# A cached-attention block whose transposing key loads are cut in two

## The chip, the cores and the metric

The kernel runs on one core of a Trainium2 chip. The metric is the device time of one execution in microseconds (us); lower is better. Three runs of the kernel before took 436.45, 436.83 and 437.62 us, with a median of 436.83 us.

On the core, TensorE (PE in the profile, with its weight loads as PEld) multiplies and transposes, VectorE (DVE) and ScalarE (ACT) work on what it leaves in PSUM, and SyncE (SP) issues every transfer between DRAM and SBUF. All transfers issued by SP run on the same 16 DMA engines.

## What is computed

Eight sequences of 112 queries attend to a cache of 512 keys and values, with 32 heads of 192 elements. Everything that is passed in is bf16.

```python
B, Sq, D = 8, 112, 640
H, Sk, Dh = 32, 512, 192
q = (x @ wq).reshape(B, Sq, H, Dh).transpose(0, 2, 1, 3)
scores = einsum("bhqd,bhkd->bhqk", q, k_cache) * Dh ** -0.5
p = softmax(scores, axis=-1)
o = einsum("bhqk,bhkd->bhqd", p, v_cache)
return o.transpose(0, 2, 1, 3).reshape(B, Sq, H * Dh) @ wo
```

The key cache and the value cache hold 8·32·512·192 elements each, 50 MB in bf16. They are read once and are most of what has to be moved.

## The kernel before

The work is cut into 32 tiles `i = 8r + b`: `r` is one of four groups of eight heads, `b` is the sequence. A tile has two steps, `n = 2i` for its first four heads and `n = 2i + 1` for the other four. `qd = n % 2` says which half a step is.

For each group of heads and each half of the batch, the `Q` operations project the queries with a piece of `wq`. Each step then runs: scores (`Sm` and `St`, line 773), the row minimum of the negated scores (`smax`, VectorE, line 830), the exponential (`exp`, ScalarE, line 835), the division by the row sum (`norm`, VectorE, line 839), the transpose of the probabilities on TensorE (`PT`, line 874), and the product with the values (`PVt` and `PVm`, lines 906 and 918). The `O` operations (line 940) multiply by a piece of `wo` and are summed in SBUF over the head groups.

For the scores the keys are needed with the 192 elements of a head on the partitions, which is not how the cache stores them. There are two ways to get there. The first seven tiles are loaded plainly (`KN`, line 189) and transposed on TensorE (`KT`, line 672). From tile 7 on, each tile of eight heads is one transposing transfer (`load_k`, line 158; in the profile `DMA_TRANSPOSE kt<-in_k_cache_dram`, 25 of them). It reads 1024 rows of 768 elements, 8·512·192·2 bytes = 1.57 MB, and writes six blocks of 1024 columns into one of `KS = 4` places of the buffer `kt`. Values come as plain copies, two to a tile with four heads each (`load_v`, line 167, 768 KB), into one of three places of `vt`. The pieces of `wq` (`WQ`, line 205, 480 KB) and `wo` (`WO`, line 216, 960 KB) are reloaded for each group of heads.

Nothing is scheduled at run time. `ORDER_PE`, `ORDER_ACT`, `ORDER_DVE` and `ORDER_SP` are lists written out in the source; each engine follows its list, and `Plan.run` puts a wait in front of an operation for each semaphore that its dependencies raise and that this engine has not waited for yet. What is late on one engine therefore holds up everything behind it in the same list.

Three rules decide when SP issues a load:

- The list `ORDER_SP`. In the part that matters it mixes keys, values and weights, often with two to four key tiles in a row: `('K', 21), ('K', 20), ('K', 22)`.
- The place. `k_place_free` makes the load of tile `i` wait for the scores of tile `i - 4`, for both of its steps, since that tile's keys lie in the place. Values wait for the product with the values three tiles earlier, weights for the operations that use their place last.
- A limit on how much is under way. Each load has a size (`size`, line 1104): a value half counts 0.5, a key tile 1.5, a `WQ` piece a third. A load waits until the latest load with at least `AHEAD = 0.95` issued behind it has landed.

On the other side, `scores(n)` waits with its first matmuls for the key load of tile `n // 2`, `PVt` for the value half of its step, `Q` for its `wq` piece.

Near the end, five steps (57 to 61) have their probabilities transposed by a transfer instead of by TensorE (`TD`, line 858).

Of the kernel before, what the change touches and what calls it, by code (L numbers as in the profile page):

```python
# [11 lines left out]
class Plan:  # L12
# [6 lines left out]
    def add(self, eng, name, deps, emit, sem=None, inc=1):  # L19
        assert name not in self.ops, name  # L20
        self.ops[name] = dict(eng=eng, deps=deps, banks=[], emit=emit, sem=sem, inc=inc)
# [31 lines left out]
def build_mha_kernel(nc, x, k_cache, v_cache, wq, wo, out):  # L53
# [4 lines left out]
    HU = 8  # L58
# [28 lines left out]
    with ExitStack() as es:  # L87
# [59 lines left out]
            return e.tensor_copy(dst, src)  # L147


        def k_place_free(i):  # L150
            return [s_last(2 * (i - KS) + 1)] if i >= KS else [("XT", c) for c in range(4)] if i == KS - 1 else []

        def load_k(i):
            r, b = divmod(i, B)

            def emit(e):
                src = k_cache[b, r * HU:(r + 1) * HU].rearrange("u (r q) d -> (u r) (q d)", q=4)
                return e.dma_start_transpose(kt[:, i % KS].rearrange("p a m c -> p (a m) c"), src)
            add("SP", ("K", i), k_place_free(i), emit, f"mK{i % KS}", 16)

        def load_v(i, half):
            r, b = divmod(i, B)
# [22 lines left out]
        def load_kn(i, lo, hi):  # L185

            def emit(e):
                b, h0 = i % B, i // B * HU
                return e.dma_start(kn[i][:, lo:hi, :], k_cache[b, h0 + lo:h0 + hi].rearrange("u (r q) d -> r u (q d)", q=4))
            if PLAIN[i] == "place":  # L190
                old = k_place_free(i)
            else:
                last = [k for k in homed(PLAIN[i]) if k < i][-1:]
                old = [("KT", k, p) for k in last for p in range(lo // 2, hi // 2)]
            add("SP", ("KN", i, lo, hi - lo), old, emit, f"mKN{i}_{lo}", 16)
            kn_of.update({(i, u): ("KN", i, lo, hi - lo) for u in range(lo, hi)})
# [33 lines left out]
        def s_last(n):  # L230
            return ("S2" if n in ROWS else "St", n, 1)

        def pv_all(n):
# [323 lines left out]
            ('KN', 0, 4, 4), ('KN', 1, 0, 4), ('KN', 1, 4, 4), ('KN', 2, 0, 4), ('KN', 2, 4, 4), ('V', 2, 0), ('V', 2, 1),  # L557
            ('V', 0, 0), ('V', 0, 1), ('WQ', 1, 0, 1), ('KN', 3, 0, 4), ('KN', 3, 4, 4), ('KN', 4, 0, 4), ('KN', 4, 4, 4),
            ('V', 1, 0), ('V', 1, 1), ('V', 3, 0), ('V', 3, 1), ('WQ', 1, 2, 1), ('WQ', 1, 1, 1), ('KN', 5, 0, 4),
            ('KN', 5, 4, 4), ('WQ', 1, 3, 1), ('KN', 6, 0, 4), ('KN', 6, 4, 4), ('V', 4, 0), ('V', 4, 1), ('K', 7),  # L560
            ('K', 8), ('WO', 0, 0), ('WO', 0, 1), ('V', 6, 0), ('V', 6, 1), ('V', 5, 0), ('V', 5, 1), ('V', 7, 0),
            ('V', 7, 1), ('K', 10), ('K', 9), ('V', 8, 0), ('V', 8, 1), ('K', 11), ('WQ', 2, 0, 1), ('V', 9, 0),
            ('V', 9, 1), ('V', 10, 0), ('V', 10, 1), ('K', 12), ('K', 13), ('V', 11, 0), ('V', 11, 1), ('K', 14),
            ('WQ', 2, 1, 1), ('WQ', 2, 2, 1), ('V', 12, 0), ('V', 12, 1), ('WQ', 2, 3, 1), ('WO', 1, 0), ('WO', 1, 1),
            ('V', 13, 0), ('V', 13, 1), ('K', 16), ('K', 15), ('V', 14, 0), ('V', 14, 1), ('V', 15, 0), ('V', 15, 1),
            ('K', 17), ('K', 18), ('K', 19), ('V', 16, 0), ('V', 16, 1), ('V', 17, 0), ('V', 17, 1), ('V', 18, 0),
            ('V', 18, 1), ('K', 21), ('K', 20), ('K', 22), ('WQ', 3, 0, 1), ('WQ', 3, 1, 1), ('V', 20, 0), ('V', 20, 1),
            ('WQ', 3, 2, 1), ('V', 19, 0), ('V', 19, 1), ('WQ', 3, 3, 1), ('WO', 2, 0), ('WO', 2, 1), ('V', 21, 0),
            ('V', 21, 1), ('V', 22, 0), ('V', 22, 1), ('K', 23), ('K', 25), ('K', 24), ('K', 26), ('V', 24, 0),
            ('V', 24, 1), ('V', 23, 0), ('V', 23, 1), ('V', 25, 0), ('V', 25, 1), ('K', 28), ('K', 27), ('K', 29),  # L570
            ('V', 27, 0), ('V', 27, 1), ('V', 26, 0), ('V', 26, 1), ('WO', 3, 0), ('WO', 3, 1), ('V', 28, 0), ('V', 28, 1),
            ('K', 30), ('K', 31), ('TD', 57), ('TD', 58), ('V', 29, 0), ('V', 29, 1), ('TD', 59), ('V', 30, 0),
            ('V', 30, 1), ('TD', 60), ('TD', 61), ('OUT', 3), ('OUT', 0), ('V', 31, 0), ('V', 31, 1), ('OUT', 5),
            ('OUT', 1), ('OUT', 2), ('OUT', 4), ('OUT', 6), ('OUT', 7)]
        BANKS = [
            (('XT', 0), 1), (('XT', 1), 4), (('XT', 3), 2), (('XT', 2), 3), (('Q', 0, 1, 1), 1), (('Q', 0, 0, 0), 5),
            (('Q', 0, 0, 1), 4), (('Q', 0, 1, 0), 6), (('KT', 0, 0), 4), (('KT', 0, 1), 0), (('Q', 0, 1, 2), 7),
# [88 lines left out]
        def k_transposes(i, p):  # L666
            bank = bank_of["KT", i, p]

            def emit(e):
                for y in range(12):  # L670
                    c, u = divmod(y, 2)
                    ends = [e.transpose(psb[:, bank + t, y * 64:(y + 1) * 64],  # L672
                                        kn[i][64 * t:64 * t + 64, 2 * p + u, c * 128:(c + 1) * 128],
                                        ident[64 * t:64 * t + 64, 64 * t:64 * t + 64]) for t in range(2)]
                return tuple(ends)

            add("PE", ("KT", i, p), [kn_of[i, 2 * p], kn_of[i, 2 * p + 1]], emit, ("PE", "PE2"))
            old = k_place_free(i) if PLAIN[i] != "place" else []
            for t in range(2):
                def evac(e, t=t):  # L680
                    dst = kt_pair(i, p).rearrange("p m (u t s) -> p m u t s", t=2, s=64)[:, :, :, t, :]
                    src = psb[:, bank + t, 0:768].rearrange("p (c u s) -> p c u s", c=6, u=2)
                    return copy(("evK", i, p, t), e, dst, src)
                add("DVE", ("evK", i, p, t), [("KT", i, p)] + old, evac)
# [82 lines left out]
        def scores(n):  # L767
# [8 lines left out]
            for j in range(2):  # L776
                def straight(e, j=j):
                    for h in range(2):
                        f = h == 0
                        if h == 0:  # L780
                            ev = [q_at(n, j, 0, 0, 64), q_at(n, j, 1, 0, 64)]
                            od = [h_at(n, j, 0, 64, 128), h_at(n, j, 1, 64, 128)]
                        else:
                            ev = [h_at(n, j, 2, 0, 64), h_at(n, j, 3, 0, 64)]
                            od = [q_at(n, j, 1, 64, 128), q_at(n, j, 2, 64, 128)]
                        for i in range(2):
                            a = mm(e, j, h, 0, ev[i], i, 0, 64, f and i == 0, False)
                            b = mm(e, j, h, 1, od[i], 1 + i, 64, 128, f and i == 0, False)
                    return a, b

                def swapped(e, j=j):
                    for h in range(2):
                        od, ev = ((h_at(n, j, 1, 0, 64), q_at(n, j, 0, 64, 128)) if h == 0 else
                                  (q_at(n, j, 2, 0, 64), h_at(n, j, 2, 64, 128)))
                        a = mm(e, j, h, 1, od, 2, 0, 64, False, True)
                        b = mm(e, j, h, 0, ev, 0, 64, 128, False, True)
                    return a, b

                def mains(e, j=j):
                    for h in range(2):  # L800
                        ev, od = ((q_at(n, j, 0, 0, 128), h_at(n, j, 1, 0, 128)) if h == 0 else
                                  (h_at(n, j, 2, 0, 128), q_at(n, j, 2, 0, 128)))
                        mm(e, j, h, 0, ev, 0, 0, 128, h == 0, False)
                        last = mm(e, j, h, 1, od, 2, 0, 128, h == 0, False)
                    return last

                def rests(e, j=j):
                    for h in range(2):
                        ev, od = ((q_at(n, j, 1, 0, 64), h_at(n, j, 0, 64, 128)) if h == 0 else
                                  (h_at(n, j, 3, 0, 64), q_at(n, j, 1, 64, 128)))  # L810
                        a = mm(e, j, h, 0, ev, 1, 0, 64, False, True)
                        b = mm(e, j, h, 1, od, 1, 64, 128, False, True)
                    return a, b
                keys = ([("evK", n // 2, 2 * qd + j, t) for t in range(2)] if n // 2 in PLAIN else [("K", n // 2)])
                if n in ROWS:
                    add("PE", ("S1", n, j), [("qc", n)] + keys, straight, ("PE", "PE2"))
                    add("PE", ("S2", n, j), [("S1", n, j)], swapped, ("PE", "PE2"))
                else:
                    add("PE", ("Sm", n, j), [("qc", n)] + keys, mains)
                    add("PE", ("St", n, j), [], rests, ("PE", "PE2"))  # L820
# [280 lines left out]

        def size(op):

            return {"V": 0.5, "WQ": op[-1] / 3, "KN": op[-1] / 8, "WO": 0.625, "K": 1.5, "X": 0.25, "TD": 0.5, "OUT": 0}[op[0]]

        for i, op in enumerate(ORDER_SP):
            behind = [k for k in range(i) if sum(map(size, ORDER_SP[k + 1:i])) >= AHEAD]
# [94 lines left out]
```

## Time and profile before

| | |
|---|---|
| median of 3 runs | 436.83 us (436.45 to 437.62) |
| the profiled execution | 438.76 us, its span 437.0 us |
| granted TensorE clock | 0.995 |
| TensorE busy | 423.3 us, 97% of the span |
| VectorE, ScalarE busy | 363.1 us, 343.7 us |
| moved by transfers | 122.04 MB, mean 279 GB/s |

The span is the time from the first to the last instruction of the program in the profiled execution; the 1.8 us between it and 438.76 us lie around the program. "Busy" for TensorE is the union of its matmuls, whose ends are modelled, so it does not mean peak rate. The DMA share that the profile gives is a mean over the 16 DMA engines; packets on one engine overlap, so a share above 1 occurs. Times inside the execution (such as 287.3 us) count from the start of the span.

### The profile page before, as it was taken

The page shows a single profiled execution, that of the slowest core. Times are in us where ns is not written, and L with a number is a line of the kernel's source. Part 1 is how long each engine was busy: PE and PEld are TensorE (multiplying, and loading weights), DVE is VectorE, ACT ScalarE, POOL GpSimd, SP SyncE. Part 2 cuts the span into 40 slices and gives each one's busy share as a digit, 9 for nine tenths or more (in the row PEclk, how much of TensorE's full clock was granted, in tenths as well). Part 3 has the DMA queues.
Part 4 walks back from the last instruction along what each step waited for, and adds up shares of the span by engine and source line. Part 5 has one row for each costly group of instructions (what it writes and reads, how often), then busy time and mean ns, then how long its engine had stood idle before and what let it go on. Part 6 is the DMA issues. An engine that isn't in the chain of part 4 may idle for free.

```text
span 437.0 us, 16234 instructions
## 1 busy us (share of the span) xinstructions
PE 423.3 (97%) x6805; PEld 290.2 (66%) x6805; DVE 363.1 (83%) x1169; ACT 343.7 (79%) x770; POOL 0.7 (0%) x6
## 2 busy tenths in 40 slices
PE   7999979999999999999999999999999999999996
PEld 4666756667677566666667666666766666576896
DVE  1479987989699889898999887889799878999872
ACT  2699979998579787988878777887878856985774
POOL 0000000000000000000000000000000000000000
PEclk9999999999999999999999999999999999999999
DMA  7998999999999999999999999999999999999972
GB/s 255 366 354 289 331 358 287 213 289 342 238 288 286 283 256 257 362 263 255 308 240 237 337 255 256 364 352 287 232 242 376 204 247 349 289 252 252 239 201 82
DMA packets 222858, 122.04 MB, mean 279 GB/s; under 512 B 165312, under 2 KB 222784, under 8 KB 222784
## 3 DMA queue, kind: packets, MB, share of 16 engines
q1 hardware_dynamic: 222784, 120.99, 106.6%
q8 instruction: 54, 0.88, 0.8%
q14 instruction: 20, 0.16, 0.1%
HBM read 78.22 MB, written 1.15 MB: 182 GB/s over the span
## 4 chain that ended last, share of the span: by engine, by line
PE 85%; DVE 7%; ACT 4%; DMA 2%; issue 1%; SPq 0%; DVEq 0%; ACTq 0%
PE ps L940 19%; PE ps L720 19%; PE ps L773 18%; PE ps L918 12%; PE ps L906 7%; PE ps L874 5%; DVE s_sb L830 4%; PE ps L672 2%; ACT p_sb L835 2%; DMA wq_sb<-in_wq_dram 2%; DVE p_sb L839 1%; ACT kt L146 1%; PE ps L973 1%; ACT qr L146 1%; DVE pT_sb L147 1%
## 5 line engine op out<-in xcount | busy, mean ns | idle before, releaser
L835 ACT ACTIVATE p_sb<-s_sb,nmx 112x512 bf16<-112x512 f32 x256 | 183.0, 718 | 32.8 <-DVE s_sb L830 25.6
L830 DVE TENSOR_SCALAR_CACHE_REDUCE s_sb<-ps 112x512 f32<-112x512 f32 x256 | 169.2, 683 | 23.3 <-PE ps L773 19.1
L720 PE MATMUL ps<-xT_sb,wq_sb 128*128 128x448 bf16 x480 | 103.2, 356 | 3.1 <-DMA wq_sb<-in_wq_dram 2.1
L773 PE MATMUL ps<-kt,qr 128*128 128x256 bf16 (+1 forms) x512 | 95.6, 273 | 1.1 <-ACT oT_sb L146 0.4
L940 PE MATMUL ps<-oT_sb,wo_sb 128*128 128x448 bf16 (+1 forms) x480 | 93.3, 341 | 0.3 <-DVE pT_sb L147 0.2
L773 PE MATMUL ps<-kt,qh 128*128 128x256 bf16 (+1 forms) x512 | 87.5, 272 | 0.0
L839 DVE TENSOR_SCALAR p_sb<-p_sb,rinv 112x512 bf16<-112x512 bf16 x256 | 81.2, 346 | 1.5
L720 PEld LDWEIGHTS ps<-xT_sb,wq_sb 128*128 128x128 bf16 x480 | 43.1, 98 | 41.9 <-DMA wq_sb<-in_wq_dram 2.8
L940 PEld LDWEIGHTS ps<-oT_sb,wo_sb 128*128 128x128 bf16 x480 | 44.3, 98 | 35.4 <-DVE pT_sb L147 0.8
L146 ACT ACTIVATE oT_sb<-ps 128x672 bf16<-128x672 f32 x64 | 46.1, 725 | 22.3 <-PE ps L918 21.7
L773 PEld LDWEIGHTS ps<-kt,qr 128*128 128x128 bf16 (+1 forms) x512 | 44.3, 96 | 25.7 <-issue 14.3
L146 ACT ACTIVATE qr<-ps 128x448 bf16<-128x448 f32 x96 | 49.7, 541 | 12.8 <-PE ps L720 12.1
L146 ACT ACTIVATE pT_sb<-ps 128x768 bf16<-128x768 bf16 x59 | 47.0, 800 | 10.3 <-PE ps L874 10.2
L918 PE MATMUL ps<-pT_sb,vt 128*128 128x112 bf16 x944 | 54.9, 213 | 0.0
L918 PEld LDWEIGHTS ps<-pT_sb,vt 128*128 128x128 bf16 x944 | 47.4, 98 | 4.1
L835 ACT ACTIVATION_READ_ACCUMULATOR p_sb<-s_sb,nmx 112x1 f32 x256 | 49.7, 194 | 0.0
L773 PEld LDWEIGHTS ps<-kt,qh 128*128 128x128 bf16 (+1 forms) x512 | 43.9, 96 | 6.1
L147 DVE COPY pT_sb<-ps 128x1024 bf16<-128x1024 bf16 x59 | 40.2, 682 | 2.4 <-PE ps L874 1.3
L874 PE MATMUL ps<-ident,p_sb 64*128 64x64 bf16 (+1 forms) x1888 | 37.4, 186 | 0.9 <-DVE p_sb L839 0.5
L874 PEld LDWEIGHTS ps<-ident,p_sb 64*128 64x128 bf16 (+1 forms) x1888 | 33.2, 94 | 6.9 <-DVE p_sb L839 2.6
L906 PE MATMUL ps<-pT_sb,vt 128*64 128x112 bf16 x944 | 32.8, 215 | 1.4 <-DVE s_sb L830 0.5
L906 PEld LDWEIGHTS ps<-pT_sb,vt 128*64 128x64 bf16 x944 | 25.5, 110 | 12.2 <-issue 3.4
(53 smaller groups left out, 228.2 us busy)
## 6 DMA issues: line engine op xcount, KB each, us to landing
vt<-in_v_cache_dram SPq DMA_DIRECT2D x64, 768.0 KB, 6.7
wo_sb<-in_wo_dram SPq DMA_DIRECT2D x8, 960.0 KB, 8.2
wq_sb<-in_wq_dram SPq DMA_DIRECT2D x14, 480.0 KB, 5.7
wo_sb<-in_k_cache_dram SPq DMA_DIRECT2D x6, 768.0 KB, 7.1
accT<-in_k_cache_dram SPq DMA_DIRECT2D x6, 768.0 KB, 7.2
vt<-in_k_cache_dram SPq DMA_DIRECT2D x2, 768.0 KB, 8.5
out_dram<-xT_sb SPq DMA_DIRECT2D x8, 140.0 KB, 2.5
wq_sb<-in_wq_dram SPq DMA_DIRECT2D x1, 960.0 KB, 7.5
```

Source lines behind the costliest of these rows:

```text
L146: return e.activation(dst, src, ACTF.Copy)
L147: return e.tensor_copy(dst, src)
L672: ends = [e.transpose(psb[:, bank + t, y * 64:(y + 1) * 64], kn[i][64 * t:64 * t + 64, 2 * p + u, c * 128:(c + 1) * 128], ident[64 * t:64 ...
L720: mm = e.matmul(ps[:, bank, 0:SG], w, v, start=(dc == 0), stop=(dc == DC - 1))
L773: return e.matmul(ps[:, 2 * j + odd, hs], q, ktb[j][lo:hi, :, blk, h * 128:(h + 1) * 128], start=first, stop=last, skip_group_check=True)
L830: return e.tensor_scalar(s_sb[:, a, :].rearrange("p (e c) -> p e c", e=2), ps[0:SQ, 2 * j:2 * j + 2, h * 256:(h + 1) * 256], -scale, None, ...
L835: return e.activation(p_sb[:, k, :], s_sb[:, a, :], ACTF.Exp, bias=nmx[:, k:k + 1], scale=-1.0, accum_out=rsum[:, k:k + 1])
L839: return e.tensor_scalar(p_sb[:, k, :], p_sb[:, k, :], rinv[:, k:k + 1], None, op0=ALU.mult)
L874: ends.append(e.transpose(psb[:, bank + t, i * w:(i + 1) * w], p_sb[lo:hi, (4 * n + k) % 8, q * 128:(q + 1) * 128], ident[lo:hi, lo:hi]))
L906: mm = e.matmul(ps[64 * h:64 * h + 64, b0 + j, SQ:2 * SQ], vtb[:, h0 + 2 * j + h, d0:d0 + 64], pT(j, h, q), start=(q == 0), stop=(q == 3))
L918: mm = e.matmul(ps[:, b0 + j, 2 * h * SQ:(2 * h + 1) * SQ], vtb[:, h0 + 2 * j + h, d0:d0 + 128], pT(j, h, q), start=(q == 0), stop=(q == 3))
L940: mm = e.matmul(ps[:, bank_of["O", g, m], 0:nc_], wo_sb[:, k, m * 128:(m + 1) * 128], oT_sb[:, g % 2, k, 0:nc_], start=(k == 0), stop=(k = ...
```

## The change

Each transposing load of eight heads becomes two loads of four heads, listed one right behind the other. The first half has the columns of heads 0 to 3 in each of the six blocks, the second half those of heads 4 to 7; each reads 512 rows (0.79 MB) and writes six blocks of 512 columns. Each half has a semaphore of its own. The step `n` waits for the half `qd` that it reads, and a half waits for the step of the old tile that read the same half of the place. In the rule on loads under way each half counts 0.75. There are 50 transposing key loads instead of 25; the order of everything else stays.

```diff
-        def k_place_free(i):
-            return [s_last(2 * (i - KS) + 1)] if i >= KS else [("XT", c) for c in range(4)] if i == KS - 1 else []
-
-        def load_k(i):
+        def k_place_free(i, half):
+
+            if i >= KS:
+                return [s_last(2 * (i - KS) + (half if "place" not in (PLAIN.get(i), PLAIN.get(i - KS)) else 1))]
+            return [("XT", c) for c in range(4)] if i == KS - 1 else []
+
+        def load_k(i, half):
             r, b = divmod(i, B)
+            u0 = half * LP
 
             def emit(e):
-                src = k_cache[b, r * HU:(r + 1) * HU].rearrange("u (r q) d -> (u r) (q d)", q=4)
-                return e.dma_start_transpose(kt[:, i % KS].rearrange("p a m c -> p (a m) c"), src)
-            add("SP", ("K", i), k_place_free(i), emit, f"mK{i % KS}", 16)
+                src = k_cache[b, r * HU + u0:r * HU + u0 + LP].rearrange("u (r q) d -> (u r) (q d)", q=4)
+                dst = kt[:, i % KS].rearrange("p a m c -> p (a m) c")[:, :, u0 * 128:(u0 + LP) * 128]
+                return e.dma_start_transpose(dst, src)
+            add("SP", ("K", i, half), k_place_free(i, half), emit, f"mK{i % KS}_{half}", 16)
...
             if PLAIN[i] == "place":
-                old = k_place_free(i)
+                old = k_place_free(i, lo // LP)
...
-            ('V', 4, 1), ('K', 7), ('K', 8), ('WO', 0, 0), ('WO', 0, 1), ('V', 6, 0), ('V', 6, 1), ('V', 5, 0), ...
+            ('V', 4, 1), ('K', 7, 0), ('K', 7, 1), ('K', 8, 0), ('K', 8, 1), ('WO', 0, 0), ('WO', 0, 1), ('V', 6, 0), ...
...
-            old = k_place_free(i) if PLAIN[i] != "place" else []
+            old = k_place_free(i, p // 2) if PLAIN[i] != "place" else []
...
-                keys = ([("evK", n // 2, 2 * qd + j, t) for t in range(2)] if n // 2 in PLAIN else [("K", n // 2)])
+                keys = ([("evK", n // 2, 2 * qd + j, t) for t in range(2)] if n // 2 in PLAIN else [("K", n // 2, qd)])
...
-            return {"V": 0.5, "WQ": op[-1] / 3, "KN": op[-1] / 8, "WO": 0.625, "K": 1.5, "X": 0.25, "TD": 0.5, "OUT": 0}[op[0]]
+            return {"V": 0.5, "WQ": op[-1] / 3, "KN": op[-1] / 8, "WO": 0.625, "K": 0.75, "X": 0.25, "TD": 0.5, "OUT": 0}[op[0]]
```

No tile of this kernel is of the kind "place", so the two other users of `k_place_free` matter only in that the plainly loaded tiles, too, get a place by halves.

## Prediction before the result

> **What bounds the kernel now.** I read the page first (busy shares, DMA share, DMA queues), then the busy time by stretches, then who waits for transfers, then single transfers against the work that needs them.
>
> ```profile
> PE 423.3 (97%) x6805; PEld 290.2 (66%) x6805; DVE 363.1 (83%) x1169; ACT 343.7 (79%) x770; POOL 0.7 (0%) x6
> DMA  7998999999999999999999999999999999999972
> q1 hardware_dynamic: 222784, 120.99, 106.6%
> ```
>
> TensorE is busy for 97% of the span, but the DMA engines are also full from the second slice to the last but two. By stretches (columns: window, length, busy time of PE, PEld, DVE, ACT, POOL, granted clock, DMA share, GB/s):
>
> ```profile
> 71.00:160.00 89.00, 87.99 (x1478) 59.44 (x1475) 78.47 (x250) 72.56 (x165) 0.00 (x0) 1.00 1.13 268
> 160.00:290.00 130.00, 129.40 (x2015) 87.94 (x2013) 114.41 (x374) 106.49 (x246) 0.00 (x0) 1.00 1.15 289
> 290.00:400.00 110.00, 109.02 (x1634) 72.41 (x1633) 98.46 (x319) 86.86 (x200) 0.00 (x0) 1.00 1.15 273
> ```
>
> From 71 us, where the transposing key loads begin, to 400 us TensorE idles 1.01 + 0.60 + 0.98 = 2.6 us in all. So no change to loads can win more than 2.6 us there. The list of waits confirms it: TensorE's waits for a transfer are two, for weights, in the first 10 us; between 71 and 400 us the only wait for a transfer is ScalarE's 1.9 us.
>
> ```profile
> PEld ps L720 <- DMA wq_sb<-in_wq_dram: 2.8, 2, 2.0
> ACT p_sb L835 <- DMA wq_sb<-p_sb: 1.9, 1, 1.9
> ```
>
> TensorE sets the pace, and the loads keep up. By how little, two places show. Each triple is the issue on SP, its time from issue to landing, and the first matmuls that need it:
>
> ```profile
> 280.13 0.37 SPq L205 DMA_DIRECT2D wq_sb<-in_wq_dram  x1
> DMA to landing us min/median/max: 6.9/6.9/6.9
> 287.32 1.12 PE L720 MATMUL ps<-xT_sb,wq_sb 128*128 128x448 bf16 x5
> ...
> 398.46 0.46 SPq L167 DMA_DIRECT2D vt<-in_v_cache_dram  x1
> DMA to landing us min/median/max: 6.3/6.3/6.3
> 407.21 0.58 PE L906 MATMUL ps<-wq_sb,vt 128*64 128x112 bf16 x16
> ```
>
> The `wq` piece lands at 287.0 and is used at 287.3: slack 0.3 us. The value half of step 59 lands at 404.8 and is used at 407.2: slack 2.4 us. Two limits thus lie almost on each other, and the slower stream of loads decides if it gets longer.
>
> **The change, part by part.**
>
> *One more boundary inside every key tile.* This is the part that counts. A transposing load against the DMA engines:
>
> ```profile
> L158 SPq DMA_TRANSPOSE kt<-in_k_cache_dram x25: 6182/7212/8611, 71.3 to 385.5; - x25
> ...
> 251.00:255.00 4.00, 4.00 (x64) 2.71 (x62) 3.00 (x11) 2.93 (x8) 0.00 (x0) 1.00 1.27 289
> 255.20:256.40 1.20, 1.20 (x8) 0.65 (x7) 1.12 (x5) 1.20 (x5) 0.00 (x0) 1.00 0.34 7
> 257.20:257.60 0.40, 0.40 (x8) 0.28 (x8) 0.40 (x2) 0.38 (x1) 0.00 (x0) 1.00 1.29 284
> 257.60:262.60 5.00, 5.00 (x89) 3.04 (x86) 4.68 (x15) 3.51 (x8) 0.00 (x0) 1.00 1.28 290
> 262.80:264.40 1.60, 1.60 (x34) 1.58 (x31) 1.52 (x8) 1.58 (x6) 0.00 (x0) 1.00 1.02 95
> ...
> 227.40:227.70 0.30, 0.30 (x4) 0.17 (x3) 0.30 (x3) 0.30 (x1) 0.00 (x0) 1.00 1.27 289
> 227.80:228.40 0.60, 0.60 (x5) 0.27 (x4) 0.60 (x3) 0.60 (x3) 0.00 (x0) 1.00 1.27 146
> 228.40:229.00 0.60, 0.60 (x5) 0.36 (x4) 0.57 (x3) 0.28 (x2) 0.00 (x0) 1.00 0.54 80
> ...
> 226.29 8.40 SPq L158 DMA_TRANSPOSE kt<-in_k_cache_dram  x1
> 254.53 6.76 SPq L158 DMA_TRANSPOSE kt<-in_k_cache_dram  x1
> ...
> q1 hardware_dynamic: 762, 0.19, 95.0%
> ```
>
> Inside a transposing load the engines move a steady 290 GB/s, so a tile of 1.57 MB needs 5.4 us. SP spends 7.2 us (median) issuing one, which I read as SP being held back by a full queue. At 227.7 one key tile ends and the next, issued at 226.29, begins: for 1.2 us the rate falls to 146 and then 80 GB/s. In that window only q1 (the row with 762 packets, from 227.6 to 229.0) moved anything, so it isn't a fetch of instructions that took the engines. At 257.4 there is the same kind of boundary and no dip (284 GB/s). The difference is in the issue: 254.53 is 2.8 us ahead of its boundary, 226.29 only 1.4 us, because the stop of 255.2 to 256.4 had given SP time. So a transfer needs more than 1.4 us from its issue until its packets flow at full rate, and the queue that SP leaves behind a transposing load holds about 1.4 us of work. A second half is issued exactly there, when SP gets free of the first.
>
> Price of one new boundary, from the two rows of the dip: 0.6·(290−146)/290 + 0.6·(290−80)/290 = 0.30 + 0.43 = 0.73 us of the stream. Lower end 0 (the 257.4 boundary). Upper end 1.1 us: at 262.8 a boundary coincides with a fetch of instructions, 1.6·(290−95)/290 = 1.08. A gain is excluded, since the same bytes pass and no row of a transposing load shows more than 290 GB/s. I take 0.73, the boundary whose issue has the same lead as the new ones.
>
> The dip is not special to key tiles; a plain value load behind a key tile shows it too (69 GB/s), so the half-to-value boundary stays as it is:
>
> ```profile
> 325.80:326.40 0.60, 0.60 (x7) 0.49 (x5) 0.34 (x1) 0.60 (x3) 0.00 (x0) 1.00 0.68 69
> ```
>
> *Where it reaches the end.* The tiles 7 to 14, before 177 us, add up to 5.8 us too; places freed early (below) hide them. If that cover is gone, up to 5.8 us come on top, 451.4 us, which the range takes in. From there to the `wq` piece at 287.3 lie eight tiles in the list (16, 15, 17, 18, 19, 21, 20, 22): 8·0.73 = 5.8 us against 0.3 us of slack. To the value half at 407.2 lie nine more: 17·0.73 = 12.4 us against 2.4 us. The later place decides, since what TensorE has already lost is part of it: 12.4 − 2.4 = 10.0 us.
>
> *Places freed by halves.* A first half can go out one step earlier. This moves the stream ahead until something else holds it; the last such thing is the fourth `wq` piece of group 2, whose place TensorE frees at 176.34:
>
> ```profile
> 174.34 2.00 PE ps L720 x10
> 177.16 0.37 SPq L205 DMA_DIRECT2D wq_sb<-in_wq_dram  x1
> DMA to landing us min/median/max: 5.7/5.7/5.7
> ...
> 134.23 0.52 SPq L205 DMA_DIRECT2D wq_sb<-in_wq_dram  x1
> DMA to landing us min/median/max: 4.0/4.0/4.0
> ```
>
> It can be issued 0.8 us earlier, and then land in 4.0 us, as at 134.23, not 5.7. So the stream is at most 0.8 + 1.7 = 2.5 us ahead at this point and at least 0, as the eight boundaries before it use the lead up. I take the middle, 1.2 us, because both rows are equally near.
>
> *Waits.* A second half must also wait for the load two in front of it (0.75 + 0.5 ≥ 0.95). For tile 21 that is a value half:
>
> ```profile
> 242.63 0.37 SPq L167 DMA_DIRECT2D vt<-in_v_cache_dram  x1
> DMA to landing us min/median/max: 6.6/6.6/6.6
> 246.81 7.67 SPq L158 DMA_TRANSPOSE kt<-in_k_cache_dram  x1
> ```
>
> It lands at 249.2, while the first half keeps SP until about 246.8 + 3.8 = 250.6: no cost, 1.4 us of cover. If that cover goes, all loads behind it in the list are late by the same amount. The second load behind a pair now waits for the pair's first half, which ends half a tile (2.7 us) before the second: no cost. On TensorE 25 odd steps get one wait more. The rows of line 773 bound it: TensorE idles 1.1 and 0.0 us in front of 1024 of its matmuls. I take 0; the upper end is 1.1 us.
>
> ```profile
> L773 PE MATMUL ps<-kt,qr 128*128 128x256 bf16 (+1 forms) x512 | 95.6, 273 | 1.1 <-ACT oT_sb L146 0.4
> L773 PE MATMUL ps<-kt,qh 128*128 128x256 bf16 (+1 forms) x512 | 87.5, 272 | 0.0
> ```
>
> Scores that start after half a tile gain nothing, as no score waits for keys.
>
> *Sum.* 10.0 − 1.2 = 8.8 us on the profiled execution, 438.8 + 8.8 = 447.6 us. That execution lies 1.9 us above the median, so the forecast for the median is 436.8 + 8.8 = 445.6 us.
>
> **The rivals.**
>
> *Every boundary costs its upper end.* Fetches of instructions wait for the end of a transposing load (the 262.8 row); twice as many ends could each catch one. 17·1.1 − 2.4 = 16.3 us, so 453 us or more. Against it: the number of fetches does not grow.
>
> A row for the next rival, a stretch of plain value loads:
>
> ```profile
> 209.20:211.30 2.10, 2.09 (x48) 1.32 (x47) 2.10 (x7) 1.38 (x5) 0.00 (x0) 1.00 1.06 391
> ```
>
> *A fixed cost for each transfer.* Should every transfer cost the stream a time of its own, 17 more of them add 17 times that, less the slack of 2.4 us. The nearest row is against it: value halves, as large as the new key halves, pass at 391 GB/s, so each takes 2.0 us with everything in it, and a fixed part must be well below 2.0 us. With half of that, 1.0 us, the time would be 436.8 + 17·1.0 − 2.4 = 451.4 us.
>
> The Trainium skill has this rule on the page "DMA: Bandwidth & Descriptors": section "Anatomy of one DMA" puts about 2.0 us of fixed cost on each transfer (measured there for transfers that GpSimd issues), and section "Bandwidth" says to batch to 1 MiB or more. By its figure the time would be, as an estimate, 436.8 + 17·2.0 − 2.4 = 468 us. The row of the value loads does not bear it out as a cost of a full stream.
>
> *No difference.* If the new boundaries are like that at 257.4, the stream takes as long as now, and TensorE sets 436.8 us as before. The point is 2.4/17 = 0.14 us for each tile, or 0.2 us with the lead of 1.2 us. For it: it is seen once in the rows above. Against it: it had a lead of 2.8 us, which the new ones lack.
>
> *A small loss.* Boundaries of 0.2 to 0.4 us, where a dip merges with a fetch that would have stopped the stream anyway: 17·0.3 − 3.6 = 1.5 us, 438.3 us.
>
> *Faster.* Fetches of instructions for TensorE that now wait behind a whole tile are served after half a tile, so TensorE starves less. All its idle time between 71 and 400 us is 2.6 us; at the very best 434.2 us. It decides only if the stream is not slowed at all.
>
> **How the numbers follow.** About 0.3% (1.3 us) is what a measurement of this kernel can tell from no change. Chances: the forecast with boundaries of 0.4 to 1.1 us 0.55 (its own range 440 to 453, as 17·0.4 − 3.6 = 3.2 and 17·1.1 − 2.4 = 16.3); the upper-end rival 0.11; a fixed cost for each transfer 0.04; a small loss 0.10; no difference 0.15; faster 0.05. Slower by over 0.3% is 0.55 + 0.11 + 0.04 + 0.10 = 0.80. The range of 437 to 456 us leaves out faster, half of no difference and half of the two dearest cases: 0.05 + 0.075 + 0.075 = 0.20.
>
> **What would show it.** Right: dips at the boundary between the halves of a tile, below 200 GB/s for about a microsecond, also where no instructions are fetched; two halves together keeping SP longer than the 7.2 us of a whole tile; TensorE waiting for `wq` pieces, value halves or `TD` transfers after 270 us, and idling about 9 us more between 270 and 420 us. Wrong: a rate of 285 to 290 GB/s across those boundaries, no wait for a transfer after 71 us, and an unchanged time. If the halves' dips are there but TensorE does not wait, the slack was larger than the two places show.

## The result, and the profile after

The changed kernel takes 457.8 us (median of 4 runs, 456.4 to 459.4) against 436.9 us before: a ratio of 1.048, with a 95% interval of 1.044 to 1.052. That is 20.9 us slower. Some executions run slower at a lower granted clock; times and ratios here leave them out. The forecast was 445.6 us, with a range up to 456 us: the direction was right, the size less than half of what came.

The profiled execution took 456.42 us, 1.4 us under the median, and its span is 454.5 us, 17.5 us more than the span before (that one lay 1.9 us above its median). The traces thus show 17.5 us of the 20.9. First the page's rows on busy shares, DMA share and queue of the kernel after:

```profile
PE 427.6 (94%) x6805; PEld 292.3 (64%) x6805; DVE 363.8 (80%) x1169; ACT 344.3 (76%) x770; POOL 0.7 (0%) x6
DMA  8999999999999999999999999999999999999872
q1 hardware_dynamic: 223584, 120.99, 104.8%
```

The same bytes pass and the engines count as full in nearly the same slices, but TensorE's share falls from 97% to 94%. By stretches (same columns as in the prediction):

```profile
71.00:160.00 89.00, 87.19 (x1454) 58.79 (x1453) 77.34 (x245) 71.91 (x164) 0.00 (x0) 1.00 1.12 261
160.00:290.00 130.00, 123.98 (x1886) 83.51 (x1885) 110.63 (x362) 101.22 (x233) 0.00 (x0) 0.98 1.11 269
290.00:400.00 110.00, 104.81 (x1619) 70.22 (x1618) 90.06 (x293) 83.27 (x190) 0.00 (x0) 0.99 1.13 272
400.00:454.00 54.00, 46.48 (x680) 35.99 (x678) 34.66 (x114) 30.63 (x69) 0.00 (x0) 0.96 0.80 195
```

TensorE now idles 1.8 + 6.0 + 5.2 us in the first three stretches, where it idled 1.0 + 0.6 + 1.0 us, and 7.5 us in the last, where it idled 3.6 us from 400 us to the end. Over the whole span it idles 13.2 us more (26.9 instead of 13.7 us). The other 4.3 us are longer busy time of the same 6805 matmuls, at a granted clock of 0.987 instead of 0.995. The moved volume per second falls most in the second stretch (269 GB/s; before, the three had 268, 289 and 273). The list of waits (total, times, longest) names what TensorE and ScalarE wait for:

```profile
ACT p_sb L843 <- DMA wq_sb<-p_sb: 7.7, 2, 7.0
PEld ps L728 <- DMA wq_sb<-in_wq_dram: 6.6, 5, 2.1
PE ps L728 <- DMA wq_sb<-in_wq_dram: 5.6, 5, 2.0
PE ps L914 <- DMA vt<-in_v_cache_dram: 1.8, 3, 1.2
```

`wq` pieces, value halves and the `TD` transfers: all three kinds that the prediction named. (The two rows of line 728 are largely the same waits, told once for the weight load and once for the matmul.) The longest wait by far is one of ScalarE. The timelines of ScalarE, TensorE and SP around it (start, duration, engine and line, in brackets the idle time before it and what ended it):

```profile
413.94 0.72 ACT L843 ACTIVATE p_sb<-s_sb,nmx 112x512 bf16<-112x512 f32 x1 [7.03 <-DMA wq_sb<-p_sb]
...
415.54 0.28 PE L781 MATMUL ps<-kt,qr 128*128 128x256 bf16 x1 [4.42 <-DVE s_sb L838]
...
403.04 0.61 DVE L847 TENSOR_SCALAR p_sb<-p_sb,rinv 112x512 bf16<-112x512 bf16 x2
...
406.01 3.49 SPq L163 DMA_TRANSPOSE kt<-in_k_cache_dram  x1
409.60 3.68 SPq L866 DMA_TRANSPOSE wq_sb<-p_sb  x2
```

The exponential of step 59 waits 7.0 us for the transfer of step 57, and TensorE stands 4.4 us behind it. VectorE had finished step 57 at 403.65; SP issued the transfer only at 409.60, when it was done with the second half of tile 31. The same wait stood in the kernel before, with 1.9 us:

```profile
397.45 0.72 ACT L835 ACTIVATE p_sb<-s_sb,nmx 112x512 bf16<-112x512 f32 x1 [1.92 <-DMA wq_sb<-p_sb]
```

So step 57's transfer landed at 397.4 and now lands at 413.9, 16.5 us later. That is nearly the whole 17.5 us of the span.

*The dips.* Two boundaries between halves of one tile in the kernel after, tile 16 at 198.0 and tile 9 at 121.3, none with a fetch of instructions. First the stretches, then the issue of the second half:

```profile
196.00:197.40 1.40, 1.40 (x9) 0.76 (x8) 1.40 (x5) 0.90 (x3) 0.00 (x0) 1.00 1.27 290
197.60:199.20 1.60, 1.60 (x10) 0.80 (x9) 1.57 (x7) 1.19 (x4) 0.00 (x0) 1.00 1.18 171
119.50:121.00 1.50, 1.50 (x10) 0.77 (x9) 1.43 (x6) 1.04 (x3) 0.00 (x0) 1.00 0.75 13
121.20:122.80 1.60, 1.60 (x12) 1.01 (x11) 1.39 (x5) 0.76 (x3) 0.00 (x0) 1.00 1.28 288
...
196.65 3.60 SPq L163 DMA_TRANSPOSE kt<-in_k_cache_dram  x1
118.50 3.93 SPq L163 DMA_TRANSPOSE kt<-in_k_cache_dram  x1
```

The half issued 1.4 us ahead of its boundary costs 1.6·(290−171)/290 = 0.66 us in that window. The half issued 2.8 us ahead, because the stream had stopped before it (13 GB/s), costs nothing. I counted the packets around all boundaries of back-to-back key loads: with a lead under 2 us, 16 without a fetch lose 0.78 us on average and 20 with one lose 1.34 us (before: 0.98 in the only one, 1.31 in ten). So the boundaries that also take a fetch rose from 10 to 20. Counted in the same way, ten boundaries in the traces of the kernel before, the kernel after, their repeats and the run with the old limit (below) had a lead of 2.2 us or more and no fetch; they lost 0.01 to 0.32 us, with a median of 0.02 us. From first to last packet, the 25 transposing loads took 179.8 us in sum before, and the 50 halves 200.7 us; at 290 GB/s both would be 135.4 us. The change costs the stream 20.9 us inside its key loads, 0.84 us for each new boundary: 6.0 us in the tiles up to 14, 14.9 us behind them.

### The profile page after: what moved, and what is told of

It reads as the page before. It is cut to its first block, busy times and chain, and to the rows that moved or that the text cites. A ratio compares the mean times of both kernels' runs of the same rounds, so it can differ in the third digit from the quotient of the medians.

```text
span 454.5 us, 16300 instructions
## 1 busy us (share of the span) xinstructions
PE 427.6 (94%) x6805; PEld 292.3 (64%) x6805; DVE 363.8 (80%) x1169; ACT 344.3 (76%) x770; POOL 0.7 (0%) x6
## 4 chain that ended last, share of the span: by engine, by line
PE 75%; DMA 9%; DVE 6%; ACT 6%; issue 2%; SPq 0%; DVEq 0%; ACTq 0%
PE ps L948 18%; PE ps L781 16%; PE ps L728 16%; PE ps L926 10%; PE ps L914 6%; DMA wq_sb<-in_wq_dram 5%; PE ps L882 5%; DVE s_sb L838 3%; ACT p_sb L843 3%; PE ps L680 2%; DMA kt<-in_k_cache_dram 2%; DMA vt<-in_v_cache_dram 1%; ACT kt L146 1%; DVE p_sb L847 1%; DMA wq_sb<-p_sb 1%
## 5 line engine op out<-in xcount | busy, mean ns | idle before, releaser
L146 ACT ACTIVATE qr<-ps 128x448 bf16<-128x448 f32 x96 | 49.8, 542 | 15.7 <-PE ps L728 15.2
```

The lines of the kernel that those rows point to most:

```text
L146: return e.activation(dst, src, ACTF.Copy)
```

## The experiments

My theory after this trace: nothing hides a boundary, early or late, and the delay of the stream reaches the end whole, because step 57's transfer lies on the path without slack. The rivals: early boundaries are hidden as predicted; the finer limit on loads under way is what holds SP; fetches or a fixed cost for each transfer make the dips.

**Only the early tiles, only the late tiles.** Whole tiles elsewhere, with the old rules.

```diff
+    HALVES = range(7, 15)        # the other run: range(15, 32)
...
+            nu = LP if i in HALVES else HU
...
+        ORDER_SP = [op for op in ORDER_SP if op[0] != "K" or op[1] in HALVES or op[2] == 0]
```

> Only the tiles 7 to 14 are cut in two; the tiles 15 to 31 stay whole, with the old rules for place, size and waits. The theory on record (places freed by halves hide the eight early boundaries) expects 436.9 us, at most 0.5 us from before. The theory formed on the trace after (the limit on loads under way, not the place, held the early halves, so no lead was gained and nothing hides a boundary; each costs the stream 0.6 to 0.8 us, which is passed on to the end because the transfer of step 57 lies on the path without slack) expects 8 times 0.65 to 0.85, so 5 to 7 us: 442 to 444 us.

> Only the tiles 15 to 31 are cut in two. The theory on record expects 436.8 + 17 times 0.73 - 2.4 = 446.8 us, without the lead. The theory formed on the trace after expects 17 times 0.84 = 14.3 us with no slack to take off, 451 us; together with the run that cuts only the early tiles it should add up to the 21 us of the whole change. If the boundaries cost far more than each alone because there are so many in a row, the two together stay well below 21 us.

Tiles 7 to 14 alone: 446.6 us against 439.2 us on that chip, ratio 1.018 (1.011 to 1.024), about 7.7 us. Tiles 15 to 31 alone: 457.5 us, ratio 1.042 (1.036 to 1.047), about 18.2 us. With the early tiles alone cut, their boundaries are not hidden; that step of the prediction falls. In the trace of the run with the early tiles alone the loads of tiles 7 to 14 take 65.3 us in sum, against 59.1 us in the kernel before as repeated on another chip (below), and the fourth `wq` piece of group 2, behind all of them, lands 4.7 us later (186.5 against 181.8): a small part is covered, and step 57's transfer lands 6.0 us later (402.7 against 396.6). The list of waits of the run with the early tiles alone shows where they arrive, at `wq` pieces that were nearly free of waits before:

```profile
PEld ps L731 <- DMA wq_sb<-in_wq_dram: 6.2, 4, 3.1
PE ps L731 <- DMA wq_sb<-in_wq_dram: 5.2, 3, 3.0
ACT p_sb L846 <- DMA wq_sb<-p_sb: 1.9, 1, 1.9
```

The early effect agrees with the 5 to 7 us of my new theory within its interval; the late one is larger than its 14.3 us. Their sum is 25.9 us.

**The change once more, on another chip**, to see if that sum contradicts the whole.

> The kernel after the change once more, beside the same runs of the kernel before. If the partial cuts add up (7.7 and 18.2 us) because each boundary costs about 1 us on this chip, the change costs 22 to 26 us here. If the first measurement stands for every chip, 20 to 21.5 us, and the partial cuts overlap by some 5 us: the early boundaries then fill waits that SP has anyway once the late ones delay the stream.

461.6 us against 439.6 us, ratio 1.048 (1.044 to 1.052), 21 to 22 us. The first measurement stands. The sum of the parts, a ratio of about 1.059, lies above it, but its own interval is about ±0.008 wide, so an overlap of the two parts is likely and not settled by the times. The traces point the same way: with the late tiles alone cut, step 57's transfer lands 16.3 us later than in the kernel before as repeated (412.9 against 396.6), nearly as late as the 16.5 us of the whole change. So the early boundaries cost about 7.7 us alone, but little on top of the late ones.

**The old limit on loads under way.** A first half counts 1.5, a second 0.

```diff
-"K": 0.75,
+"K": 1.5 * (op[-1] == 0),
```

> All 25 tiles are cut in two, but the limit on loads under way counts a first half as 1.5 and a second half as 0, so that each load waits for the same earlier load as in the kernel before. If the new boundaries alone cost the time, it stays within 1 us of the 457.8 us of the change. If the finer limit (a second half waits for the load two in front of it) holds SP and opens gaps, it comes out 2 us or more faster than the change.

Ratio 1.047 (1.040 to 1.054), the same as the change; a gain of the expected 2 us or more is not excluded by this interval alone. In this run, too, a second half has a wait that no load had before, for the load right in front of its pair. The traces show that it holds next to nothing: from the end of a first half's issue to the start of the second's, SP loses more than 0.15 us at one tile of 25, 0.53 us in the kernel after and 0.63 us in this run. So the second halves are hardly held, and the finer limit is not the main cause.

**Stripped to the key loads.** Only `load_k` is left, in wholes, halves and quarters.

```diff
+                for h in range(PARTS):
+                    if t >= KS:
+                        e.wait_ge(sk[t % KS][h], 16 * (t // KS))
+                    e.dma_start_transpose(dst, src).then_inc(sk[t % KS][h], 16)
```

> All work is left out but the 25 transposing key loads of the tiles 7 to 31, whole, issued one behind the other on SP, each waiting only for the load that used its place four tiles before. Nearly no instructions are fetched and nothing else is moved. If a boundary costs the stream about 0.75 us because the next load is issued only 1.4 us ahead, the loads take 25 times 5.42 + 24 times 0.75 = 153.5 us from the first packet to the last. If the dips come from fetches of instructions or from the other transfers, they vanish here and it takes 135.5 us.

> The same with halves, 50 loads. Issue lead: 135.4 + 49 times 0.75 = 172.2 us, 18.7 us more than with whole tiles; each boundary seen with a lead of 1.4 to 1.5 us and without any fetch. Fetches or other transfers as the cause: 135.5 us as with whole tiles. A fixed cost of 2.0 us for each transfer: 135.4 + 49 times 2.0 = 233 us.

> The same with quarters, 100 loads of two heads each. If the price is one of the boundary and does not depend on the size, 135.4 + 99 times 0.75 = 209.7 us. If SP, with loads this short, gets ahead of the stream, so that a quarter is already queued whole when the one before it ends, the price falls and it takes less than 190 us.

From first to last packet: 159.2, 182.5 and 190.0 us. The steady stretch of each run (whole tiles, halves, quarters; the last column is GB/s):

```profile
10.00:150.00 140.00, 0.00 (x0) 0.00 (x0) 1.00 1.16 247
```

```profile
10.00:175.00 165.00, 0.00 (x0) 0.00 (x0) 1.00 1.08 215
```

```profile
10.00:185.00 175.00, 0.00 (x0) 0.00 (x0) 1.00 1.16 207
```

The dips are there with no fetches and no other traffic. Halving costs 23.3 us for 25 new boundaries, 0.93 us each. Cutting again costs 7.5 us for 50 more, 0.15 us each. So the cost is no fixed price of the transfer or of the boundary. It falls with the lead: among the boundaries of the quarters, 20 with less than 1.6 us lose 0.66 us on average, and 16 with 2.0 us or more lose 0.33 us. What is the same in all three runs is the queue. These rows count q1's packets between the issue of one load and its boundary, for one load of each run in the same order (packets, MB, share of the engines):

```profile
q1 hardware_dynamic: 1471, 0.37, 116.1%
```

```profile
q1 hardware_dynamic: 1450, 0.36, 114.6%
```

```profile
q1 hardware_dynamic: 1563, 0.39, 113.2%
```

SP is let go when about 1500 packets are left. At full rate that is 1.3 us; I measured leads of 1.4 to 1.5 us with wholes and halves. With quarters of 1536 packets the 1500 include the dip of the boundary in between, so the lead grows to 1.77 us on average (up to 2.2) and the mean loss falls to 54.5/99 = 0.55 us.

**Keys and values in turn**, to see a boundary whose next load is queued early.

```diff
+                    e.dma_start(vt[:, t % VS, v0:v0 + 4], vsrc).then_inc(sv[t % VS][h], 16)
```

> Key halves and value halves alternate on SP, 50 of each, everything else is left out. A value half is issued in 0.4 us, so the key half behind it is issued while the value half still flows, about 3.4 us ahead of its own boundary. Issue lead: only the boundaries behind key halves cost 0.75 us, 50 times (2.71 + 2.0) + 50 times 0.75 = 273 us. A fixed cost for each transfer of 0.75 us, whatever its lead: 235.5 + 99 times 0.75 = 310 us.

292.1 us, about midway between the two, so the total decides for neither. The single boundaries do better. One pair of boundaries: a key half ends at 64.3, the value half at 67.6.

```profile
61.80:63.80 2.00, 0.00 (x0) 0.00 (x0) 1.00 1.24 280
64.10:65.30 1.20, 0.00 (x0) 0.00 (x0) 1.00 0.87 138
65.30:66.90 1.60, 0.00 (x0) 0.00 (x0) 1.00 1.02 360
66.90:67.70 0.80, 0.00 (x0) 0.00 (x0) 1.00 1.45 223
...
62.81 0.58 SPq L45 DMA_DIRECT2D vt<-in_v_cache_dram  x1
63.44 5.39 SPq L39 DMA_TRANSPOSE kt<-in_k_cache_dram  x1
```

Behind the key half, issued 1.3 us ahead, the rate drops to 138 GB/s for 1.2 us. Behind the value half, with the key half queued 3.4 us ahead, it only passes from one rate to the other. Averaged over all pairs the first costs about 0.9 us and the second about 0.2 us. The lead and the order of the two kinds of load change together here, so this run alone does not tell them apart; the boundaries between two key loads with a long lead (above) do.

**A second queue for the values**, stripped and in the whole kernels (before and after).

```diff
-        order["POOL"], order["SP"] = ORDER_POOL, ORDER_SP
+        by_pool = [op for op in ORDER_SP if op[0] == "V" and op[1] >= 7]
+        order["POOL"] = ORDER_POOL + by_pool
+        order["SP"] = [op for op in ORDER_SP if op not in by_pool]
...
+        ORDER_SP = order["SP"]        # only where POOL is outside the limit
```

> Stripped loads: 50 key halves on SP and 50 value halves on POOL's own queue at the same time, waiting only for their places; everything else is left out. With both on SP one behind the other they took 292 us from the first packet to the last, 240 us of it at full rate. If a boundary is a stretch with too little queued, the second queue fills it: 240 to 260 us. If it is a stop of the engines or of the path for transposing, it stays at 285 us or more.

> The kernel after the change, with the values of the tiles 7 to 31 issued by POOL on a queue of its own, in the same order and with the same waits for places and for loads under way; keys and weights stay on SP. If a boundary is a stretch in which nothing else is queued, value packets fill it wherever a value half may be under way beside the keys, and a good part of the 21 us comes back: below 450 us. If the boundary occupies the DMA engines or the transposing path itself, the time stays at 457 us or more.

> The kernel before the change with the same move of its values to POOL. TensorE sets its pace and idles 2.6 us between 71 and 400 us, so filled dips can win that at the most and the 1.9 us of the wait for step 57: 433 to 437 us. If POOL is slow to issue 512 pieces of 1.5 KB for each value half, or the values delay the keys, it gets slower than 437 us.

> The kernel after the change with the values of the tiles 7 to 31 on POOL's queue, now outside the limit on loads under way, so that they wait only for their places. If the limit (a value half waits until keys listed ahead of it have landed, and keys behind it wait for the values) cost the 38 us of the first try, it falls below the 457.8 us of the change; if values and keys at once delay the keys that are needed next, or POOL is slow in issuing, it stays above 470 us.

Stripped: 287 us from first to last key packet, not the 240 to 260 us expected of filled dips. The stretch and the two queues while both run, and SP's issue:

```profile
20.00:120.00 100.00, 0.00 (x0) 30.04 (x40) 1.00 1.05 372
...
q0 software_dynamic: 8545, 34.96, 93.4%
q1 hardware_dynamic: 8939, 2.27, 11.1%
...
4.07 64.58 SPq L50 DMA_TRANSPOSE kt<-in_k_cache_dram  x2
```

The engines run at 372 GB/s. The two boundaries between key halves in this stretch, at 48 and 84 us, still show, but only as a microsecond at about 300 GB/s instead of 380, about 0.2 us each: a second queue mostly fills them. But in 100 us POOL's values move 34.96 MB and the keys 2.27 MB; two key halves hold SP for 64.6 us. In number of packets the queues are even (8545 and 8939); the value packets are 16 times as large. The keys then run alone, with all their dips. In the whole kernels the move costs time: with POOL within the limit the kernel before goes to 474.2 us (ratio 1.079, 1.070 to 1.089) and the kernel after to 495.6 us (1.128, 1.121 to 1.136), and without the limit the kernel after takes 540 us or more. Within the limit a key half of the kernel after still lands in a median of 7.2 us; TensorE's longest waits for a transfer are for `wq` pieces, 20.8 us in all instead of 5.6. Without the limit the key halves are late as well. The row of DMA issues of that run (median us to landing, 7.2 in the kernel after):

```profile
kt<-in_k_cache_dram SPq DMA_TRANSPOSE x50, 11.3
```

**Quarters in the whole kernel.**

```diff
+        ORDER_SP = [q for op in ORDER_SP for q in ([("K", op[1], 2 * op[2]), ("K", op[1], 2 * op[2] + 1)] if op[0] == "K" else [op])]
```

> The whole kernel with every transposing key load cut in four loads of two heads, 100 instead of 25; a quarter counts 0.375 in the limit, places are freed by halves, scores wait for both quarters of their half. If each boundary has a price of its own of 0.84 us, 75 new ones cost 63 us: 500 us. If the price comes from the lead, which SP's queue gives in packets (about 1460 are left when a load has been issued, nearly a whole quarter) and which grows in time when dips stretch them, the stripped loads say 0.15 us for each of the 50 further boundaries: 7 to 10 us more than with halves, 465 to 470 us.

479.1 us against 438.8 us, ratio 1.090 (1.083 to 1.096), about 39 us: between the two expectations. From first to last packet the loads take 223.3 us in sum, against 180.8 us with whole tiles in the run below: 42.5 us for 75 new boundaries, 0.57 us each (stripped, 190.0 − 159.2 = 30.8 us, 0.41 us each). A fixed price of 0.84 us is refuted here too. What I had mis-sized was the step from halves to quarters: (42.5 − 20.9)/50 = 0.43 us for each of the 50 further boundaries, where the stripped loads gave 0.15. Why they cost more in the whole kernel is not shown.

**The end of the list.** Three orders around tile 31, and the kernel before once more for its trace.

```diff
 after, TD between the halves:   ('K', 31, 0), ('TD', 57), ('TD', 58), ('K', 31, 1), ('V', 29, 0), ('V', 29, 1), ('TD', 59), ...
 before, only tile 31 in halves: the same list
 before, values first:           ('V', 29, 0), ('V', 29, 1), ('TD', 57), ('TD', 58), ('K', 31, 0), ('TD', 59), ('K', 31, 1), ('V', 30, 0), ...
 before, last order:             ..., ('TD', 59), ('V', 30, 0), ('V', 30, 1), ('K', 31, 1), ('TD', 60), ...
```

> The kernel after the change, with the two transposing transfers of the steps 57 and 58 listed between the two halves of tile 31 instead of behind them. In the trace after the change step 57 is normalised at 403.4 us, but SP issues its transfer only at 409.6 us, behind the second half of tile 31; between the halves it could go at 405.9 us. If the delay of the stream reaches the end through this transfer, the time falls by about 3.6 us, to 454.2 us. If the values behind it set the end, or TensorE itself does, it stays at 457.8 us within 1 us.

> The kernel before the change with tile 31 alone cut in two, and the transposing transfers of the steps 57 and 58 listed between its halves. One boundary costs the stream 0.8 to 0.9 us, but the transfer of step 57, for which ScalarE waits 1.9 us in the kernel before, is issued about half a tile earlier. If that wait sets the end: 1 to 1.9 us faster than before, 435 to 436 us. If what is behind it in the list (the values of step 58, the transfer of step 59) takes its place, no gain, or 1 us slower.

> The kernel before the change once more, for its trace on the same chip as the three others. Both theories: the dips at the boundaries of whole tiles (about 0.9 us, 1.3 us with a fetch) as in the first trace, 437 to 440 us.

> The kernel before the change with a new order at the end of SP's list and tile 31 alone in halves: the values of step 58 and 59 ahead of the transfers of steps 57 and 58, then the first half of tile 31, the transfer of step 59, and the second half. If the transfers of the steps 57, 59 and 61 follow one another through ScalarE and VectorE and this chain sets the end, the first of them lands about 2 us and the second about 3 to 4 us earlier: 435 to 437 us against 438.6 us before. If the halves of tile 31 come too late for the steps 62 and 63, or TensorE itself sets the end, there is no gain or a loss of up to 3 us.

> The last order of SP's list, with the second half of tile 31 moved once more: behind the values of step 60 and 61 instead of in front of them. In the run before it, step 57's transfer landed 1.4 us earlier than in the kernel before and the values of step 59 were used 1.7 us earlier, and then step 60's transfer landed 4.3 us later, behind the half of tile 31 and the values. If the transfers of the steps 57 to 61 are the path at the end, the 1.7 us now last: about 437 us against 438.7 us before. If step 63 then waits for its keys, or step 60's transfer is held by the half in front of it, it is as slow as before or up to 4 us slower.

The first gains nothing, where 3.6 us were expected (ratio 1.051, 1.047 to 1.054, against the change's 1.048): in its trace step 59's transfer lands 13.9 us behind step 57's instead of 10.3. With tile 31 alone in halves the kernel before loses 5.4 us (ratio 1.012, 1.009 to 1.016), although only one boundary is new. Its timelines of SP and TensorE show why:

```profile
392.06 5.22 SPq L869 DMA_TRANSPOSE wq_sb<-p_sb  x2
397.37 3.12 SPq L165 DMA_TRANSPOSE kt<-in_k_cache_dram  x1
400.58 1.08 SPq L174 DMA_DIRECT2D vt<-in_v_cache_dram  x2
402.72 4.40 SPq L869 DMA_TRANSPOSE wq_sb<-p_sb  x1
...
411.13 0.40 PE L917 MATMUL ps<-wq_sb,vt 128*64 128x112 bf16 x4 [3.72 <-DMA wq_sb<-p_sb]
```

The second half, moved out of the way of step 57, now stands in front of step 59, whose transfer lands at 411.1 instead of 406.9. With the values first, step 57's transfer lands 1.4 us earlier and the values of step 59 are used 1.7 us earlier, as expected; then step 60's transfer lands 4.3 us later, and the kernel takes 445.2 us against 438.8 us (ratio 1.014, 1.010 to 1.018). The last order takes 441.3 us against 439.6 us, ratio 1.003 (1.001 to 1.005): again step 60's transfer is held, until 411.98, by the half in front of it. (The kernel before, repeated for its trace, took 438.6 us.) So the `TD` transfers of steps 59 and 60 are on the path in these orders, as that of step 57 is in the kernel after; step 58's was not moved alone. What is put in front of one of them comes out as time, though not in full. None of these orders beats the kernel before.

## Why the prediction was wrong

*TensorE sets the pace, the loads just keep up.* Right until 390 us, wrong behind it. I took the 2.4 us of slack of one value half as the last place that counts. The row that I had quoted, ScalarE's wait of 1.9 us for a `TD` transfer, said that this transfer was already late for ScalarE in the kernel before. It had no slack: 16.5 us later, it makes the span 17.5 us longer, so nothing should have been taken off.

*One more boundary costs 0.73 us because its issue has only 1.4 us of lead.* The mechanism was right, and the stripped loads show it alone. The size was 0.84 us, partly because 20 of the 36 boundaries with little lead also take a fetch (1.34 us). For the 17 late tiles the loads themselves give 14.9 us instead of 12.4. With these tiles alone cut, the forecast's terms are 10.0 us and the kernel lost 18.2 us.

*Eight early boundaries are hidden, and places freed by halves put the stream 1.2 us ahead.* Counted in the order of the list, as in the sum below, this was the largest error; by the runs with a part of the tiles it costs 7.7 us alone and about 3 us on top of the late tiles (18.2 of 20.9 us). Places did come free earlier: of the eight early tiles, five (7, 8, 10, 11, 14) were issued within 0.1 us of their place in the kernel before, and in the kernel after each of the eight first halves waited for something else, at least 6 us after its place was free. So the first half of tile 10 went out 2.1 us earlier. But that was all the lead; by tile 14 it had turned into 2.9 us of delay, and SP issued the fourth `wq` piece of group 2 at 179.31 instead of 177.16. The issues on SP, before (tiles 10 and 14):

```profile
108.38 6.67 SPq L158 DMA_TRANSPOSE kt<-in_k_cache_dram  x1
161.61 8.61 SPq L158 DMA_TRANSPOSE kt<-in_k_cache_dram  x1
```

and after (tiles 10 and 14, and the `wq` piece with its time to landing):

```profile
106.26 4.66 SPq L163 DMA_TRANSPOSE kt<-in_k_cache_dram  x1
164.51 4.67 SPq L163 DMA_TRANSPOSE kt<-in_k_cache_dram  x1
179.31 0.37 SPq L210 DMA_DIRECT2D wq_sb<-in_wq_dram  x1
DMA to landing us min/median/max: 7.1/7.1/7.1
```

An earlier place is a lead only up to the next hold. For tile 10 that is the limit on loads under way: its first half goes out 0.1 us after the value half three places ahead in the list has landed, at 106.18. The piece landed at 186.4 instead of 182.8, 3.6 us later, where I had forecast 1.2 us earlier.

*Waits cost nothing.* Borne out as far as tried: with the old limit the time is the same within about 3 us, and a second half is held once, for 0.5 us. TensorE's waits for halves and the rule for places by halves were not undone by themselves.

*The sum.* Forecast 8.8 us. Up to the `wq` piece 4.8 us were missed (3.6 instead of −1.2). From there to step 57's transfer the delay grew by 12.9 us, from 3.6 to 16.5, where I had 12.4 − 2.4 = 10.0: 2.5 us more for the price, 2.4 us of slack that was not there, less 2.0 us by which the delay grew less than the loads did (14.9 us). With the late tiles alone cut, this part of the delay is 15.2 us, from 1.1 us at the `wq` piece to 16.3; so the 2.0 us look like early delay that is made up again; in which waits was not traced. 8.8 + 4.8 + 2.9 = 16.5 us, and 1.0 us more comes behind it. The remaining 3.4 us between the traces and the medians are where the two profiled executions lie among their runs.

*The rivals.* The upper-end rival (1.1 us each, 453 us) came nearer to the time and was half right: twice as many boundaries did catch a fetch, though the stripped loads show that most of a dip needs none. The fixed cost (451.4 us) came nearer for the wrong reason: stripped, quarters cost only 0.15 us more for each further boundary. The Trainium skill's 2.0 us for each transfer ("DMA: Bandwidth & Descriptors", section "Anatomy of one DMA") would have given an estimated 468 us; no run here shows it as a cost of a queue that is kept full. The stripped halves, estimated at 233 us by that figure, took 182.5 us. No difference, a small loss and faster are refuted.

## What to carry to other kernels

A transposing load issued behind another one on the same queue has only the lead that the queue leaves it, so cutting such loads smaller costs time: here 0.84 us for each cut of a tile in halves, 0.57 us for each cut in quarters. In a kernel whose loads just keep up this reaches the end. Before slack is taken off a delay, look for the waits for transfers that already exist: a wait of 1.9 us in the list says that there is none at that place. And an earlier free place is a lead only as far as the next thing that holds the same load.

## What was not expected of the hardware

Where TensorE stood for 4.4 us, its granted clock was lower afterwards (windows of the kernel after; the column ahead of the last two is the clock):

```profile
405.00:410.80 5.80, 5.80 (x55) 3.51 (x50) 4.56 (x14) 0.73 (x1) 0.00 (x0) 1.00 1.17 246
415.50:420.00 4.50, 4.46 (x38) 2.46 (x39) 4.01 (x14) 2.18 (x6) 0.00 (x0) 0.62 0.96 326
420.00:425.00 5.00, 5.00 (x83) 3.74 (x82) 3.66 (x12) 3.56 (x10) 0.00 (x0) 1.00 1.07 279
```

At 0.62 over 4.5 us, 1.7 us of clock are lost. Shorter waits in the same trace were followed by the same: after 1.5 us that ended at 248.1 us the granted clock was 0.50 from 248.5 to 251.9 us, and after 2.0 us that ended at 289.6 us it was 0.51 from 289.5 to 292.9 us. After a wait of 1.6 us that ended at 281.4 us it stayed at 1.00, so these rows give no length of wait from which on it happens. How much of the lost clock reaches the time was not tried. And in the stripped run two queues shared the engines by packets, not by bytes: 8545 packets of POOL's queue against 8939 of SP's in the same 100 us, 34.96 MB against 2.27 MB.
